# A token-mixing and expert-layer kernel: a new order of work for the first batch

## Chip, cores and metric

The kernel runs on one core of one Trainium2 chip. The metric is the device time of one execution in microseconds (us). Several executions of the same kernel are timed and the median is taken. One further thing is known of each kernel: a profile of one execution, with a record of every instruction on each engine. The engines are named as in the profile: PE (TensorE matmuls), PEld (its weight loads), DVE (VectorE), ACT (ScalarE), POOL (GpSimd) and SP (SyncE, which here only issues DMAs).

## What is computed

```python
X = np.fft.rfft(x, axis=1)                 # x: (8, 3008, 256)
Y = X * (filt_r + 1j * filt_i)[None]       # filters: (1505, 256)
y = np.fft.irfft(Y, n=3008, axis=1)        # (8, 3008, 256)
h = y.reshape(24064, 256) @ w_in           # w_in: (256, 2048)
g = h * (1 / (1 + np.exp(-beta * h)))      # beta: (2048,)
out = g @ w_out                            # (24064, 256), float32
```

## The kernel before

**The Fourier part.** 3008 is 47 times 64, so the transform is done in two stages of matmuls with tables. `t1` (94x96) is the first stage, `t2` (24 tables of 128x128) the second; the spectrum is multiplied with the filters on DVE; `t3` (24 tables of 128x128) and `t4` (96x94) take it back. `t3s` is `t3` with its two halves exchanged and a sign put on each row ("rotated"). The tables are computed on the chip: GpSimd writes index tiles (`iota`), DVE turns them into phases, ACT takes the sine.

**The expert part.** Blocks of 512 tokens, 47 of them. For each of 16 slices of the 2048 inner columns there is one step: two matmuls into `hps` (L719), one Silu on ACT (L728), and two steps later four matmuls into `acc` (L739). There are 752 steps. While the steps of one batch run, the Fourier stages of the next batches are put between them: a plan (`at`, L645) says at which step which matmul of which batch is issued (functions `s1`, `s2`, `s3`, `s4`).

**The first batch** has no steps to hide behind. It runs alone before step 0, in an order written out by hand (L298 to L542), with its own functions: `s1_0(g)` (first stage, 8 groups of 4 columns of x, evacuated into `aT` on DVE or ACT), `a0_turn` (PE transposes of `aT` into `a0`), `t3_part` (transposes of `t2` into `t3`), `t3_rotate` (from `t3` to `t3s`), `s2_0(n)` (second stage of unit n, and its two products `pq_t` with the filters on DVE, L423), `s3_0(n)` (back, evacuated into `zT`), `z_turn` (transposes into `zz0`), `f_0` and `s4_0` (last stage, evacuated into `ys[0]`). There are six units n, each 8 of the 24 tables by one half of the 256 columns. `spin` is a run of matmuls whose result nobody reads.

**Queues.** Each engine runs its instructions in the order of the program. The DMAs of x (float32 in memory, bfloat16 in SBUF) are issued by POOL, in the same order as its `iota`s and copies; so are half of the filter loads (`load_filters(nc.gpsimd, ...)`, L185), w_in (L480) and x of the next batch (`load_x`, L347). The other half of the filters, w_out (`load_wout`) and all later stores and loads are issued by SP. A filter half lands in 32 of 64 rows; `spread(n)` (two POOL copies, L455 and L456) makes the second 64 rows that the products of unit n need. The SP filter loads stand behind a tiny DMA `seen` (L189) that reads the second group of x.

**x in two transfers.** A batch of x is laid out as 94 rows of 32 times 256 values. Each load is two DMAs, of 80 and of 14 rows (L170 and L171, L351 and L352).

PSUM in this stage: `spsum` has 3 buffers of two banks (`bank2`), `tpsum` 2 buffers of one bank (`turn8`, `f_0`, `spin`). A matmul into a buffer waits until the engine that evacuates it is done.

Of the kernel before, what the change touches and what calls it, by code (L numbers as in the profile page):

```python
# [10 lines left out]
P = 128  # L11

ACT = mybir.ActivationFunctionType
ALU = mybir.AluOpType
ENG = mybir.EngineType
F32 = mybir.dt.float32
# [20 lines left out]
def kernel(  # L37
# [104 lines left out]
    def iota(tile_, pattern, base=0, ch=0):  # L142
        nc.gpsimd.iota(tile_, pattern=pattern, base=base, channel_multiplier=ch)
# [6 lines left out]
    ip = sp.tile([P, 1], I32, name="ip", tag="ip")  # L150
    warm = small("warm")
    nc.vector.memset(warm[:], 0.0)
    nc.scalar.activation(warm[:], warm[:], ACT.Sin)

    r_sr = ExitStack()
# [4 lines left out]

    r_sq = ExitStack()
    sq = rpool("setup_x", r_sq, bufs=1)
    x0 = sq.tile([NP, J, D], BF16, name="x0", tag="x0")
    xv0 = x[0].rearrange("(p j) d -> p j d", j=J)
    kc = sq.tile([P, NK, 2], I32, name="kc", tag="kc")
    cc = sq.tile([P, NK, 2], I32, name="cc", tag="cc")
    vi = sq.tile([P, NK, M], I32, name="vi", tag="vi")

    def load_x0(j0, j1):
        nc.gpsimd.dma_start(x0[:80, j0:j1, :], xv0[:80, j0:j1, :])  # L170
        nc.gpsimd.dma_start(x0[80:, j0:j1, :], xv0[80:, j0:j1, :])  # L171

    load_x0(0, 8)
    iota(ip[:], [[0, 1]], ch=1)
# [3 lines left out]
    iota(vi[:, :, :H], [[1, NK], [N1, H]])  # L178
    load_x0(16, 24)
    iota(vi[:, :, H:], [[1, NK], [-N1, H]], base=N1 * (M - 1))  # L180
    make_identity(nc, ident)
    load_x0(24, 28)
    load_x0(28, 32)
    for part in parts:
        load_filters(nc.gpsimd, *part)  # L185
    with nc.allow_non_contiguous_dma(reason="2048 values, once"):
        nc.sync.dma_start(beta_sb[:], moe_beta.rearrange("(fb fp) -> fp fb", fp=P))
    seen = sp.tile([1, 2], BF16, name="seen", tag="seen")
    nc.sync.dma_start(seen[:], x0[:1, 8, :2])  # L189
    for part in parts:  # L190
        load_filters(nc.sync, *part)

    def shift_and(name, sh, mask):
        t = small(name, I32)
        if sh:
# [47 lines left out]
    def s1_0(g, engines):  # L243
        ps = bank2([P, NDC, 512])
        for e in range(NDC):
            for i in range(MG):
                nc.tensor.matmul(
                    ps[:, e, i * KP : (i + 1) * KP],
                    lhsT=x0[:, g * MG + i, e * P : (e + 1) * P],
                    rhs=t1[:],  # L250
                    start=True,
                    stop=True,
                )
# [7 lines left out]
    def spin(j, n):  # L261
        ps = tpsum.tile([P, 512], F32, name="tps", tag="tps")
        for _ in range(n):
            nc.tensor.matmul(
                ps[:], lhsT=x0[:, j, :P], rhs=x0[:, j : j + 2, :], start=True, stop=True
            )

    def a0_turn(kg, e, on_act):
        tp = turn8()
# [22 lines left out]
    def turn_t4():  # L292
        tp = turn8()
        nc.tensor.transpose(tp[:KP, 0, :NP], t1[:], ident[:NP, :NP])
        nc.scalar.activation(t4[:], tp[:KP, 0, :NP], ACT.Copy)
        nc.gpsimd.tensor_scalar(t4[0:4], t4[0:4], 0.5, None, ALU.mult)

    t1v = t1[:].rearrange("p (k q) -> p k q", q=2)  # L298
    t2_half(0)
    for q in range(2):  # L300
        nc.vector.tensor_scalar_mul(t1v[:, :, q], sn[:NP], q_p[q][:NP])
    t2_half(1)
    s1_0(0, (False,))
    s1_0(1, (True,))
    spin(0, 3)
    t2_shift(0)
    t2_shift(1)
    nc.vector.memset(t2[:, 0, M : P : M - 1], 0.0)
    nc.scalar.activation(warm[:], ms[:], ACT.Silu)
    s1_0(2, (False,))  # L310
    s1_0(3, (True,))
    t3_part(0, True)
    turn_t4()
    v_i = shift_and("v_i", 5, 1)
    rot = (affine("rot0", v_i, 2.0, -1.0), affine("rot1", v_i, -2.0, 1.0))
    sgn = affine("sgn", c_i, -2.0, 1.0)
    c10 = sp.tile([P, P], BF16, name="c10", tag="c10")
    for c in range(2):
        nc.vector.tensor_copy(c10[:, c * M : (c + 1) * M], t2[:, 0, (1 - c) * M : (2 - c) * M])
    s1_0(4, (False,))  # L320
    s1_0(5, (True,))
    s1_0(6, (False,))
    s1_0(7, (False, True))
    t3_part(1, True)
    t3_rotate(1, KH, False)
    a0_turn(0, 0, False)
    a0_turn(1, 0, True)

    r_sq.close()

# [14 lines left out]
    wstage = {}  # L345

    def load_x(b, g):  # L347
        xv = x[b].rearrange("(p j) d -> p j d", j=J)
        t = xpool.tile([NP, JG, D], BF16, name="xg", tag="xg")
        js = slice(g * JG, (g + 1) * JG)  # L350
        nc.gpsimd.dma_start(t[:80], xv[:80, js, :])  # L351
        nc.gpsimd.dma_start(t[80:NP], xv[80:NP, js, :])  # L352
        xg[b, g] = t

    def load_wout(f0):
# [103 lines left out]
    def f_0(e, u, on_act):  # L459
# [14 lines left out]
            inv_scale,  # L474
        )

    spread(0)
    spread(1)
    spread(2)
    nc.gpsimd.dma_start(win_sb[:], moe_w_in.rearrange("(dc p) f -> p dc f", p=P))  # L480
# [8 lines left out]
    load_x(1, 3)  # L489
    load_wout(0)  # L490
    load_wout(WG)

    s2_0(0)
    t3_part(2, True)
    tp0 = turn8()
    nc.tensor.transpose(tp0[:, 0, :], c10[:], ident[:])
    nc.scalar.activation(t3s[:, 0, :], tp0[:, 0, :], ACT.Copy, scale=sgn[:])
    s2_0(1)
    a0_turn(2, 0, True)
    t3_rotate(KH, 2 * KH, True)  # L500
    s3_0(0)
    s2_0(2)
    a0_turn(0, 1, True)
    t3_rotate(2 * KH, NK, True)
    s3_0(1)
    s2_0(3)
    a0_turn(1, 1, True)
# [2 lines left out]
    a0_turn(2, 1, True)  # L510
    z_turn(0, 0, True)
    z_turn(0, 1, True)
    f_0(0, 0, True)
    f_0(0, 1, True)
    s3_0(3)
    s2_0(5)
    z_turn(0, 2, True)
    f_0(0, 2, True)
    f_0(0, 3, True)
    z_turn(0, 3, True)  # L520
    s3_0(4)
    f_0(0, 4, True)
    tiny = sp.tile([P, NFB], F32, name="tiny", tag="tiny")
    nc.gpsimd.tensor_tensor(tiny[:], beta_sb[:], beta_sb[:], ALU.mult)
    nc.gpsimd.tensor_scalar(tiny[:], tiny[:], 1e-12, None, ALU.is_lt)
    nc.gpsimd.tensor_scalar(tiny[:], tiny[:], 2e-6, None, ALU.mult)
    nc.gpsimd.tensor_tensor(beta_sb[:], tiny[:], beta_sb[:], ALU.add)
    f_0(0, 5, True)
    s3_0(5, True)
    f_0(0, 6, False)  # L530
    f_0(0, 7, True)
    z_turn(1, 0, False)
    z_turn(1, 1, True)
    s4_0(1, 0, False)
    z_turn(1, 2, False)
    s4_0(1, 1, True)
    z_turn(1, 3, False)
    nc.vector.reciprocal(rbeta_sb[:], beta_sb[:])
    scale_wout(0)
    scale_wout(WG)  # L540
    s4_0(1, 2, True)
    s4_0(1, 3, False)  # L542
    r_p0.close()
    r_sr.close()
    right.close()
# [14 lines left out]
    def s1(b, i, on_act):  # L560
        g, jj = divmod(2 * i, JG)
        if jj == 0:
            st["a1", b] = apool.tile([KP, JG, D], BF16, name="a1", tag="a1")
        ps = fpsum.tile([P, 512], F32, name="ps1", tag="f")
        nc.tensor.matmul(  # L565
            ps[:KP], lhsT=t1[:], rhs=xg[b, g][:, jj : jj + 2, :], start=True, stop=True
        )
        evac(st["a1", b][:, jj : jj + 2, :], ps[:KP], on_act)

# [218 lines left out]
```

## Time and profile before

| | |
|---|---|
| six runs, median (lowest to highest) | 791.58 us (789.74 to 793.6) |
| the profiled execution, its own time | 792.72 us |
| its span, first to last instruction | 790.9 us |
| PE, ACT, DVE, POOL busy, share of the span | 96%, 71%, 55%, 22% |
| first matmul of step 0 | 48.81 us |
| last first-batch DMA of x landed | 15.92 us |
| first spectrum product `pq_t` | 20.90 us |

The profile is read in stages. The time from 0 to 48.81 us is the first batch alone; from there on the steps run. The table of stretches gives for each stretch the busy time of every engine, the granted TensorE clock and the busy share of the 16 DMA engines. The chain is the line of work that ended last, each piece the one that released the next.

### The profile page before, as it was taken

What the parts mean: (1) busy time and instruction counts of PE and PEld (TensorE: products, weight loads), DVE (VectorE), ACT (ScalarE), POOL (GpSimd) and SP (SyncE); (2) the same over time, 40 slices, a digit from 0 to 9 for tenths busy, and PEclk for the clock granted to TensorE, in tenths of its full rate; (3) what the DMA queues carried; (4) which work ended last, traced back from release to release, by engine and by line L of the source; (5) the groups of instructions that cost most, each with busy time, mean ns of one, the idle gap of its engine ahead of it and who ended that gap; (6) DMA issues with size and microseconds to landing.
All of it is one profiled execution on the core that took longest, in us unless ns stands there. A gap on an engine that the chain in (4) does not pass through costs nothing.

```text
span 790.9 us, 15158 instructions
## 1 busy us (share of the span) xinstructions
PE 763.0 (96%) x5953; PEld 547.0 (69%) x6045; DVE 436.8 (55%) x683; ACT 561.8 (71%) x826; POOL 172.6 (22%) x195
## 2 busy tenths in 40 slices
PE   4789999999999999999999999999999999999997
PEld 4666767766677666776678666786667776676665
DVE  6754845676556765576655666566655566330100
ACT  4877877766667666767667766677666777777776
POOL 8925410233102321122201222012200222000000
PEclk9999999999999999999999999999999999999999
DMA  9948375441941339313581335803154211500101
GB/s 172 228 130 198 104 194 144 108 108 58 233 135 48 87 89 241 96 48 97 126 239 52 82 99 127 226 27 114 48 179 115 74 47 48 154 28 27 54 27 54
DMA packets 87530, 88.28 MB, mean 112 GB/s; under 512 B 6150, under 2 KB 78342, under 8 KB 87460
## 3 DMA queue, kind: packets, MB, share of 16 engines
q1 hardware_dynamic: 82420, 72.37, 30.7%
q0 software_dynamic: 5040, 14.95, 11.1%
q8 instruction: 47, 0.77, 0.4%
q14 instruction: 23, 0.19, 0.1%
HBM read 54.01 MB, written 46.66 MB: 127 GB/s over the span
## 4 chain that ended last, share of the span: by engine, by line
PE 93%; ACT 2%; DMA 2%; POOL 1%; issue 1%; DVE 1%; POOLq 0%; ACTq 0%
PE acc L739 42%; PE hps L719 38%; PE ps L565 3%; PE ps L632 3%; PE ps L610 3%; PE ps L581 2%; DMA a<-d 1%; DMA x<-in_x_dram 1%; ACT zz L113 1%; ACT a L113 0%; POOL x L170 0%; PE sps L432 0%; PE tps L386 0%; ACT t3s L288 0%; POOL x L171 0%
## 5 line engine op out<-in xcount | busy, mean ns | idle before, releaser
L728 ACT ACTIVATE gT<-hps,beta_sb 128x512 bf16<-128x512 f32 x752 | 516.7, 687 | 209.3 <-PE hps L719 188.5
L739 PE MATMUL acc<-wout_sb,gT 128*128 128x256 bf16 x3008 | 453.3, 272 | 2.5
L719 PE MATMUL hps<-y,win_sb 128*128 128x512 bf16 (+7 forms) x1636 | 428.2, 350 | 1.3 <-DVE y L117 1.0
L739 PEld LDWEIGHTS <-gT 128*128 128x128 bf16 x3008 | 287.5, 98 | 126.2 <-issue 1.2
L600 POOL TENSOR_TENSOR yh<-a_t,b_t 128x512 bf16<-128x512 f32 x84 | 106.3, 1266 | 415.0 <-DVE b_t L599 414.2
L719 PEld LDWEIGHTS <-win_sb 128*128 128x128 bf16 x1728 | 164.9, 98 | 25.3 <-issue 1.3
L115 DVE COPY ost<-acc 128x512 f32<-128x512 f32 x93 | 59.9, 685 | 146.9 <-PE acc L739 146.9
L115 DVE CAST a<-ps 96x512 bf16<-96x512 f32 x104 | 70.9, 685 | 51.9 <-PE ps L565 47.9
L595 DVE TENSOR_TENSOR a_t<-ps,fr_sb 128x512 f32<-128x512 f32 x84 | 58.1, 691 | 72.0 <-PE ps L581 70.9
L117 DVE TENSOR_SCALAR y<-ps 128x376 bf16<-128x376 f32 x104 | 55.9, 547 | 59.3 <-PE ps L632 59.1
L596 DVE SCALAR_TENSOR_TENSOR b_t<-ps,fi_sb 64x512 f32<-64x512 f32 x84 | 58.2, 692 | 1.1
L599 DVE TENSOR_TENSOR b_t<-ps,fi_sb 64x512 f32<-64x512 f32 x84 | 57.4, 683 | 1.1
L115 DVE CAST z<-ps 128x512 bf16<-128x512 f32 x72 | 49.3, 684 | 1.7 <-PE ps L610 0.8
L632 PEld LDWEIGHTS <-zz 96*128 96x128 bf16 x448 | 29.8, 98 | 22.9 <-DMA zz<-d 0.2
L565 PE MATMUL ps<-xg,t 94*96 94x512 bf16 x112 | 41.5, 381 | 0.6
L632 PE MATMUL ps<-t,zz 96*128 96x94 bf16 x448 | 34.7, 205 | 0.8
L581 PE MATMUL ps<-a,t 128*128 128x256 bf16 x168 | 32.1, 273 | 1.1 <-DMA a<-d 0.8
L610 PE MATMUL ps<-yh,t 128*128 128x256 bf16 x168 | 32.1, 273 | 0.6
L351 POOL DMA_DIRECT2D xg<-in_x_dram x28 | 15.2, 542 | 63.3 <-PE ps L565 63.3
L610 PEld LDWEIGHTS <-t 128*128 128x128 bf16 x168 | 16.3, 98 | 17.7
L581 PEld LDWEIGHTS <-t 128*128 128x128 bf16 x168 | 16.1, 98 | 16.0 <-issue 1.1
L565 PEld LDWEIGHTS <-t 94*96 94x96 bf16 x112 | 13.8, 123 | 10.5
(100 smaller groups left out, 204.8 us busy)
## 6 DMA issues: line engine op xcount, KB each, us to landing
out_dram<-ost SPq DMA_DIRECT2D x46, 512.0 KB, 3.0
d<-a SPq DMA_DIRECT2D x28, 384.0 KB, 4.4
a<-d SPq DMA_DIRECT2D x28, 384.0 KB, 5.3
d<-z SPq DMA_DIRECT2D x28, 384.0 KB, 3.7
zz<-d SPq DMA_DIRECT2D x28, 384.0 KB, 7.0
xg<-in_x_dram POOLq DMA_DIRECT2D x28, 320.0 KB, 5.8
ws<-in_moe_w_out_dram SPq DMA_DIRECT2D x4, 512.0 KB, 14.6
xg<-in_x_dram POOLq DMA_DIRECT2D x28, 56.0 KB, 5.8
```

Of the source, the lines that this page charges most:

```text
L115: nc.vector.tensor_copy(dst, src)
L565: nc.tensor.matmul(ps[:KP], lhsT=t1[:], rhs=xg[b, g][:, jj : jj + 2, :], start=True, stop=True)
L581: nc.tensor.matmul(ps[:, e, :], lhsT=t2[:, k0 + e, :], rhs=st["a2", b, g][:, kk + e, :], start=True, stop=True,)
L595: nc.vector.tensor_tensor(a_t[:], ps[:], fr_sb[:, ks, :], ALU.mult)
L596: nc.vector.scalar_tensor_tensor(b_t[:M], ps[M:], -1.0, fi_sb[M:, ks, :], ALU.mult, ALU.mult)
L599: nc.vector.tensor_tensor(b_t[M:], ps[:M], fi_sb[M:, ks, :], ALU.mult)
L600: nc.gpsimd.tensor_tensor(yh[:], a_t[:], b_t[:], ALU.add)
L610: nc.tensor.matmul(ps[:, e, :], lhsT=t3[:, 2 * i + e, :], rhs=yh[:, e, :], start=True, stop=True)
L632: nc.tensor.matmul(ps[:, e, :NP], lhsT=zz[:, j0 % JG + e, dc * P : (dc + 1) * P], rhs=t4[:], start=True, stop=True,)
L719: nc.tensor.matmul(hps[:, pos - t0 : pos - t0 + ln], lhsT=win_sb[:, dc, fb * P : (fb + 1) * P], rhs=ys[b][:, dc, n0 : n0 + ln], start=(dc ...
L728: nc.scalar.activation(gT[:], hps[:], ACT.Silu, scale=beta_sb[:, fb : fb + 1])
L739: nc.tensor.matmul(acc[tb // 2][:, tb % 2, :], lhsT=gT[:, tb * P : (tb + 1) * P], rhs=wout_sb[:, fb, :], start=(fb == 0 and tb % 2 == 0), ...
```

## The change

It leaves the steps as they are, but for one entry of the plan, and rewrites the first batch in these points:

- a bfloat16 tile `rest` of zeros; `spin(17)` on it ahead of all matmuls, and `spin(4)` where `spin(0, 3)` was;
- x in single DMAs of 96 rows (the last two rows are those of the next batch, and no matmul reads them), for the first batch and for all others but the last;
- the identity after the fourth x load; the fourth and fifth filter parts on POOL not ahead of the spreads but just before `spread(0)` and `spread(1)`; `seen` on SP reads `t2`, so that the SP filter loads start when `t2` is nearly done;
- the two writes of `t1` on ACT instead of DVE;
- the work on `beta` on DVE early, and `scale_wout` after the last x load on POOL;
- `t3_part(1)` and `t3_part(2)` earlier; the second of three `t3_rotate` on DVE, right before the products, the third stays on ACT;
- another order of `s3_0(3)`, `s2_0(5)`, `z_turn` and `f_0`; the last two `z_turn` become one `z_pair` into a two-bank buffer;
- in the plan of batch 1, the first `s2` at step 19 instead of 18.

```diff
+    rest = sp.tile([P, 512], BF16, name="rest", tag="rest")
+    nc.vector.memset(rest[:], 0.0)
...
+    def load_rows(t, b, j0, j1):
+        if b + 1 < B:
+            src = AP(x.tensor, x.offset + (b * S + j0) * D, [[J * D, KP], [D, j1 - j0], [1, D]])
+            nc.gpsimd.dma_start(t, src)
+        else:
...
     def load_x0(j0, j1):
-        nc.gpsimd.dma_start(x0[:80, j0:j1, :], xv0[:80, j0:j1, :])
-        nc.gpsimd.dma_start(x0[80:, j0:j1, :], xv0[80:, j0:j1, :])
+        load_rows(x0[:, j0:j1, :], 0, j0, j1)
...
+    load_x0(24, 28)
     make_identity(nc, ident)
-    load_x0(24, 28)
     load_x0(28, 32)
-    for part in parts:
+    for part in parts[:3]:
         load_filters(nc.gpsimd, *part)
...
-    seen = sp.tile([1, 2], BF16, name="seen", tag="seen")
-    nc.sync.dma_start(seen[:], x0[:1, 8, :2])
-    for part in parts:
-        load_filters(nc.sync, *part)
...
+    spin(17)
     t1v = t1[:].rearrange("p (k q) -> p k q", q=2)
+    for q in range(2):
+        nc.scalar.activation(t1v[:, :, q], sn[:NP], ACT.Copy, scale=q_p[q][:NP])
     t2_half(0)
-    for q in range(2):
-        nc.vector.tensor_scalar_mul(t1v[:, :, q], sn[:NP], q_p[q][:NP])
     t2_half(1)
     s1_0(0, (False,))
     s1_0(1, (True,))
-    spin(0, 3)
+    spin(4)
...
     nc.vector.memset(t2[:, 0, M : P : M - 1], 0.0)
+    seen = sp.tile([1, 2], BF16, name="seen", tag="seen")
+    nc.sync.dma_start(seen[:], t2[:1, 1, P - 2 :])
+    for part in parts:
+        load_filters(nc.sync, *part)
...
-    turn_t4()
...
+    nc.vector.reciprocal(rbeta_sb[:], beta_sb[:])
     s1_0(4, (False,))
     s1_0(5, (True,))
+    t3_part(1, True)
     s1_0(6, (False,))
+    turn_t4()
     s1_0(7, (False, True))
-    t3_part(1, True)
     t3_rotate(1, KH, False)
     a0_turn(0, 0, False)
     a0_turn(1, 0, True)
+    t3_part(2, True)
+    t3_rotate(KH, 2 * KH, False)
...
+    load_filters(nc.gpsimd, *parts[3])
     spread(0)
+    load_filters(nc.gpsimd, *parts[4])
     spread(1)
...
+    scale_wout(0)
+    scale_wout(WG)
 
     s2_0(0)
-    t3_part(2, True)
...
+    a0_turn(2, 0, True)
     s2_0(1)
-    a0_turn(2, 0, True)
-    t3_rotate(KH, 2 * KH, True)
+    t3_rotate(2 * KH, NK, True)
     s3_0(0)
...
-    t3_rotate(2 * KH, NK, True)
...
+    s3_0(3)
+    s2_0(5)
     f_0(0, 0, True)
     f_0(0, 1, True)
-    s3_0(3)
-    s2_0(5)
     z_turn(0, 2, True)
+    z_turn(0, 3, True)
     f_0(0, 2, True)
     f_0(0, 3, True)
-    z_turn(0, 3, True)
...
-            s23_steps(1, [o + r for r in (18, 21, 23, 26, 28, 30, 34, 36, 39, 41, 44, 46)], 5, 1)
+            s23_steps(1, [o + r for r in (19, 21, 23, 26, 28, 30, 34, 36, 39, 41, 44, 46)], 5, 1)
```

`z_pair(e, hh, engines)` does the transposes of two `z_turn`s into one buffer of `spsum`, and evacuates the two halves on the two engines given.

More of the change, by code (lines that the diff above doesn't have):

```diff
@@ L162 @@
     sq = rpool("setup_x", r_sq, bufs=1)
-    x0 = sq.tile([NP, J, D], BF16, name="x0", tag="x0")
-    xv0 = x[0].rearrange("(p j) d -> p j d", j=J)
+    x0 = sq.tile([KP, J, D], BF16, name="x0", tag="x0")
     kc = sq.tile([P, NK, 2], I32, name="kc", tag="kc")
@@ L167 @@
     vi = sq.tile([P, NK, M], I32, name="vi", tag="vi")
+    def load_rows(t, b, j0, j1):
[3 more added lines that the diff above has]
+        else:
+            xv = x[b].rearrange("(p j) d -> p j d", j=J)
+            nc.gpsimd.dma_start(t[:80], xv[:80, j0:j1, :])
+            nc.gpsimd.dma_start(t[80:NP], xv[80:NP, j0:j1, :])
     def load_x0(j0, j1):
-        nc.gpsimd.dma_start(x0[:80, j0:j1, :], xv0[:80, j0:j1, :])
-        nc.gpsimd.dma_start(x0[80:, j0:j1, :], xv0[80:, j0:j1, :])
+        load_rows(x0[:, j0:j1, :], 0, j0, j1)
     load_x0(0, 8)
@@ L248, in s1_0 @@
                     ps[:, e, i * KP : (i + 1) * KP],
-                    lhsT=x0[:, g * MG + i, e * P : (e + 1) * P],
+                    lhsT=x0[:NP, g * MG + i, e * P : (e + 1) * P],
                     rhs=t1[:],
@@ L259, in s1_0, with spin @@
                 evac(aTv[:, g, e], src[:, e], engines[e])
-    def spin(j, n):
+    def spin(n):
         ps = tpsum.tile([P, 512], F32, name="tps", tag="tps")
         for _ in range(n):
-            nc.tensor.matmul(
-                ps[:], lhsT=x0[:, j, :P], rhs=x0[:, j : j + 2, :], start=True, stop=True
-            )
+            nc.tensor.matmul(ps[:], lhsT=rest[:, :P], rhs=rest[:], start=True, stop=True)
     def a0_turn(kg, e, on_act):
@@ L319 @@
         nc.vector.tensor_copy(c10[:, c * M : (c + 1) * M], t2[:, 0, (1 - c) * M : (2 - c) * M])
+    tiny = sp.tile([P, NFB], F32, name="tiny", tag="tiny")
+    nc.vector.tensor_tensor(tiny[:], beta_sb[:], beta_sb[:], ALU.mult)
+    nc.vector.tensor_scalar(tiny[:], tiny[:], 1e-12, 2e-6, ALU.is_lt, ALU.mult)
+    nc.vector.tensor_tensor(beta_sb[:], tiny[:], beta_sb[:], ALU.add)
+    nc.vector.reciprocal(rbeta_sb[:], beta_sb[:])
     s1_0(4, (False,))
     s1_0(5, (True,))
+    t3_part(1, True)
     s1_0(6, (False,))
+    turn_t4()
     s1_0(7, (False, True))
-    t3_part(1, True)
     t3_rotate(1, KH, False)
@@ L347, in load_x @@
     def load_x(b, g):
[L348 to L352, printed above, removed]
+        t = xpool.tile([KP, JG, D], BF16, name="xg", tag="xg")
+        load_rows(t[:], b, g * JG, (g + 1) * JG)
         xg[b, g] = t
@@ L475, in f_0, with z_pair @@
         )
+    def z_pair(e, hh, engines):
+        tp = spsum.tile([P, 2, KH, P], BF16, name="sps", tag="sps")
+        for h in range(2):
+            for i in range(KH):
+                j0 = ((hh + h) * KH + i) * KP
+                nc.tensor.transpose(tp[:, h, i, :], zT[e][:, j0 : j0 + P], ident[:])
+        for h in range(2):
+            evac(zz0[:, (hh + h) * KH : (hh + h + 1) * KH, e * P : (e + 1) * P], tp[:KP, h], engines[h])
+    load_filters(nc.gpsimd, *parts[3])
     spread(0)
+    load_filters(nc.gpsimd, *parts[4])
     spread(1)
@@ L512 @@
     z_turn(0, 1, True)
+    s3_0(3)
+    s2_0(5)
     f_0(0, 0, True)
     f_0(0, 1, True)
-    s3_0(3)
-    s2_0(5)
     z_turn(0, 2, True)
+    z_turn(0, 3, True)
     f_0(0, 2, True)
     f_0(0, 3, True)
-    z_turn(0, 3, True)
     s3_0(4)
     f_0(0, 4, True)
[L523 to L527, printed above, removed]
     f_0(0, 5, True)
@@ L533 @@
     z_turn(1, 1, True)
+    z_pair(1, 2, (False, True))
     s4_0(1, 0, False)
-    z_turn(1, 2, False)
     s4_0(1, 1, True)
[L537 to L542, printed above, removed]
+    s4_0(1, 2, False)
+    s4_0(1, 3, True)
     r_p0.close()
@@ L565, in s1 @@
         nc.tensor.matmul(
-            ps[:KP], lhsT=t1[:], rhs=xg[b, g][:, jj : jj + 2, :], start=True, stop=True
+            ps[:KP], lhsT=t1[:], rhs=xg[b, g][:NP, jj : jj + 2, :], start=True, stop=True
         )
```

## Prediction

> **What bounds the kernel now.** I read the table of stretches first, because the shares over the span mix two stages.
>
> ```profile
> 15.00:20.00 5.00, 3.42 (x38) 3.05 (x39) 2.13 (x5) 1.72 (x3) 3.09 (x6) 0.68 1.12 235
> 20.00:25.00 5.00, 3.99 (x62) 3.55 (x61) 4.10 (x4) 4.38 (x7) 4.77 (x5) 0.98 1.10 230
> 35.00:40.00 5.00, 4.02 (x52) 3.80 (x50) 2.35 (x2) 3.28 (x5) 3.87 (x9) 0.78 1.05 191
> 45.00:50.00 5.00, 3.51 (x47) 2.51 (x45) 3.57 (x6) 2.46 (x4) 2.55 (x2) 1.00 0.00 0
> 100.00:760.00 660.00, 655.48 (x5024) 467.94 (x5104) 369.17 (x575) 466.78 (x685) 112.72 (x113) 1.00 0.39 106
> ```
>
> Columns: stretch, length, then busy us of PE, PEld, DVE, ACT, POOL, the granted clock, DMA share, GB/s. From 100 to 760 us PE is busy 655.48 of 660 at clock 1.00: no edit here removes a matmul of the steps, so that stage stays. In the first 50 us no engine is full; there the order of work decides. So second comes the chain in order of time (start, us, what):
>
> ```profile
> 9.50 0.51 POOL x L170
> 10.02 5.90 DMA x<-in_x_dram
> 16.05 0.52 PE sps L247 x8
> 16.59 0.57 DVE aT L115
> 17.18 0.49 ACT aT L113
> ...
> 23.63 1.22 ACT t3s L288 x2
> ...
> 26.68 1.22 ACT t3s L288 x2
> ...
> 34.19 1.71 PE sps L432 x16
> ...
> 41.02 0.91 PE sps L432 x16
> ...
> 47.82 0.95 DVE y L117
> 48.81 0.59 PE hps L719 x2
> ```
>
> Read: POOL issues x until 10.02, the last x lands 5.90 later, then DVE and ACT evacuate, then ACT carries the chain (with four rotations), then PE at half speed (1.71 against 0.91 for the same 16 matmuls), and a tail of 6.9 us from the last `s3_0` to step 0. Third, the timeline around two waits:
>
> ```profile
> 18.64 1.01 PE L272 MATMUL tps<-ident,aT 128*128 128x128 bf16 x8 [0.33 <-ACT t L113]
> 19.84 1.03 POOL L455 COPY fr_sb<-fr_sb 64x1024 f32<-64x1024 f32 x1
> 21.96 0.61 PE L272 MATMUL tps<-ident,aT 128*128 128x128 bf16 x8 [0.54 <-ACT t L113]
> 68.55 0.38 PE L581 MATMUL ps<-a,t 128*128 128x256 bf16 x2 [0.84 <-DMA a<-d]
> ```
>
> The first spread starts only at 19.84, because POOL was still issuing filters, and POOL then copies without a gap to 35.89. The last row is the one stall of the early steps: 0.84 us at step 18.
>
> **x.** Ahead of the last x DMA, four issues of 14 rows go (0.53 + 0.51 + 0.86 + 0.51); the last issue then ends near 7.6 instead of 10.65. The data do not come that fast: with x alone on the queues the stretches of 4 to 8 us moved about 200 GB/s, so 1.57 MB (two more rows of 94 are 2%) take 7.9 us from 3.3, and the first group landed about 0.9 us after its share had moved; so x is in at 12.1 instead of 15.92. Here the Trainium skill ("DMA: Bandwidth & Descriptors", Anatomy of one DMA) gives each such DMA a fixed 2.0 us beside its bytes: five fewer would then be worth 10 us. The rows show the DMA engines already at share 1.03 to 1.10 at 5 to 8 us, so the fixed parts overlap; I take the issue and the bytes. This costs the filters: the SP ones start at about 11 instead of 8.44.
>
> **DVE and ACT to the end of the first stage.** The index `ip` comes 0.53 earlier, and the two `t1` writes (0.91) leave DVE for ACT, which is idle then (ACT waits 1.46 at 6.87). The zero memset precedes `ip` and is hidden. So `t2` is ready at 11.53 - 1.3 = 10.2. From there DVE is the late engine: `aT` 0.85, small ops and `c10` 0.7, four new ops on `beta` about 0.8 (POOL took 0.22 to 0.27 each), `aT` 0.9, 0.85 and 0.55: 14.85, then ACT's half 0.5: **15.35 against 17.67**. Of 3.8 us that x is earlier, 2.3 are used.
>
> **POOL.** `t4` is turned on ACT at 13.95; POOL scales it (0.47), issues two filter DMAs (0.59 each) and spreads from **15.7, against 19.84**. Two issues of filters (1.2) come between spreads 0 and 1, two of x (1.1) go: the last spread ends at 32.05 against 35.89. The filters must be there. After x is through at 11.2, the 3.15 MB of both halves take 13.7 us at the 230 GB/s of the rows above: the first pairs (128 KB each) land near 14 to 15, the last between 25.8 and 26.7, and spread 4 needs them at 27.15. That is the thinnest cover of the sum. Without it each us of lateness goes to the products, after 1.7 us of slack (below). The moved w_out scaling (2 x 1.89 on POOL) lies behind the last spread and is needed only at step 2; its cost is nothing, as DVE and ACT don't wait for it.
>
> **Rotations.** One pair leaves ACT, where it stood on the chain (1.22), for DVE. A DVE rotation took 0.34, so 0.65, and the first product comes at 17.2 (20.90 before). The rule of the skill against this: "SBUF — State Buffer", section "SBUF: two separate sides", says of the port pair that DVE and GpSimd share that a DVE instruction in a two-port mode and a GpSimd one block each other whole. By it each rotation waits for a spread copy of 1.04, and the first product is at 18.5; the row of 4.09, a DVE op on 128x48 that took 0.97 until an `iota` of POOL ended, agrees. The unit after it waits for its spread until 21.15 either way, so the sum keeps nothing of this.
>
> **ACT to the last `s3_0`.** With ACT ops of 1024 elements 0.92 apart: `a0` 15.95, `t3` 16.9, `t3s` 17.8, `a0` 18.4, rotation 19.3 to 20.55, `zT(0)` to 21.5, `a0` to 22.4, `zT(1)` (waits for spread 1) to 24.1, `a0`, `zT(2)`, `a0` to 27.2, two `zz` to **29.1 (33.7 before)**. With `s3_0(3)` and `s2_0(5)` ahead of `f_0`, ACT's wait of 1.22 at 35.94 and most of 0.57 at 37.53 go; `zT(3)` 30.0, two `y` 31.0, two `zz` 32.9, two `y` 33.9, `zT(4)` 35.1; PE does `s3_0(5)` at 34.9 to **35.8, against 41.9**. The last product is ready at 33.2 (the 1.7 of slack). The tail I work out again with `z_pair`: 6.9, as before, since the last `zz` on ACT waits for DVE's. Step 0 so starts at 42.7, 6.1 earlier. x of batch 1 lands last near 42, and its first use of that part is six steps later.
>
> **Clock.** A 128x512 matmul took 0.63 at 8.95 (cold, though the clock column shows 1.00 before its first record) and 0.38 at 48.81. PE worked from 7.71 and the x matmuls went from 281 to 206 ns at 13.1. 17 spins cost 7.3 us cold (0.43 each); started at 1.3 they end between 6.7 and 8.6, where t1 and x are ready at 6.1; DVE reaches the first `aT` at 7.5. Gain or loss on the path: -0.5 to +1.1, taken at 0. The clock fell at 16.9 and 33.9, each time after a stretch with PE waiting. The new order has such stretches too (29 to 33). A cold window cost, at 34 to 37, 1.0 (16 matmuls of L432 in 1.91 for 0.91), 0.45 (L418, 1.06 for 0.61) and 0.34 (L386, 0.95 for 0.61); I take **one, at 1.2**, the rest lying beside ACT; ends 0 and 3.5 (two).
>
> **Step 19.** The stall of 0.84 goes. But three `s2` then come in six steps, and DVE needs 2.07 for each, so the third `s3` can come 0.2 to 0.3 late: +0.6 net.
>
> **Sum:** 6.1 - 1.2 + 0.6 = 5.5. The profiled execution took 792.72 (span 790.9): it would be 787.2 (785.4). It lay 1.14 above the median, so the median goes from 791.58 to 786.1.
>
> **Rivals.** *The clock holds:* no cold window, 6.7 saved, 784.9. For: the spins bring it up early. Against: PE still waits for ACT. *The filters are late:* x first means 3.1 MB of filters from 11 us on, and a filter DMA of 256 KB took 9.6 to 14.0 to land. If spread 4 starts 4 us late, minus the slack, 2.2 are lost: 788.3. For: the SP loads start 2.6 later, and the DMA share is above 1 throughout. Against: what lands earlier frees the queue for them. In the same place falls the case that x is not earlier at all, because bytes and not issues set it. *The other side, the clock stays down:* if transposes and zero operands don't hold the clock, the stage from 18.4 on has 37 groups of 8 matmuls at 0.86 (the cold row at 35.59) = 32 us, plus some 3 us of evacuation that nothing hides: step 0 at 53.4, 4.6 later, less the 0.6 of step 19: 795.6. It decides from about 60% of the stretch 18 to 43 cold. The skill ("TensorE: Matmul & The Clock Gate", Part 4) says that transposes don't count as busy; the rows speak against it: transposes took 1.01 at 18.64 and 0.61 at 21.96, and 43 to 48 is half transposes at clock 1.00.[...]
>
> **Chances.** Forecast 0.48; clock holds 0.20; filters late 0.20; clock down 0.06; else 0.06. 0.3% (2.4 us) is about what a measurement can tell from no change. Faster: the first two and 0.6 of the third, 0.80. Within: the rest of it and most of the unnamed, 0.13. Slower: 0.07. The range reaches from the warm case with a short spin (-0.5), no late `s3` (-0.25) and `beta` ops at half their price (-0.4), 783.8, to filters late with one cold window more (+1.2), 789.5.
>
> **What would show it.** Right: `t2` copies done near 10.2, x in by 12.5, first spread before 16.5, first product near 17.3, step 0 at 43 to 44, no wait of L581 on a DMA. Wrong: x still landing at 15; POOL's spreads waiting for DMAs; clock 0.50 in more than one window after 20; step 0 later than 46; or steps that run slower than 742.1 us from first to end.

## The result, and the profile after

| | before | changed |
|---|---|---|
| median of all runs (lowest to highest, runs) | 790.79 us (788.4 to 796.68, 66) | 786.95 us (785.44 to 789.52, 29) |
| the profiled execution, its own time | 792.72 us | 787.16 us |
| its span | 790.9 us | 785.4 us |
| first matmul of step 0 | 48.81 us | 42.37 us |
| from there to the end of the span | 742.1 us | 743.0 us |

The ratio is 0.9952, with the interval 0.9942 to 0.9962: 3.8 us faster. The spans of the profiled executions differ by 5.5 us, the number of the forecast. The 1.7 between the two is the first thing to explain: the profiled execution of before lay 1.9 us above the median of its 66 runs, that of the changed kernel 0.2 above its own.

The table of stretches of the changed kernel, with the columns as before:

```profile
15.00:20.00 5.00, 4.51 (x56) 4.23 (x53) 4.92 (x7) 3.24 (x5) 4.77 (x7) 0.66 1.16 239
35.00:40.00 5.00, 4.36 (x74) 3.82 (x70) 2.57 (x5) 3.53 (x7) 3.02 (x2) 1.00 1.07 215
45.00:50.00 5.00, 5.00 (x27) 2.94 (x26) 2.61 (x4) 3.77 (x8) 0.00 (x0) 0.85 0.63 182
100.00:760.00 660.00, 655.48 (x5023) 468.02 (x5104) 368.13 (x572) 466.31 (x683) 103.15 (x96) 1.00 0.39 106
```

Read: at 15 to 20 us all three of DVE, ACT and POOL have gained work that used to come later (DVE 4.92 for 2.13, POOL 4.77 for 3.09); 45 to 50 belongs to the steps now. The stretch at half clock at 15 to 20 is still there. That of 35 to 40 is gone (1.00 for 0.78), but a new one stands at 43.5 to 46.8, inside the steps (0.85 in the third row). In the long stretch PE is busy for 655.48 us in both.

The chain in order of time (start, us, what):

```profile
10.26 0.09 DVE aT L115
...
12.07 0.19 DVE beta_sb L329
12.28 0.25 DVE rbeta_sb L330
12.54 2.14 DVE aT L115 x3
...
20.32 1.22 ACT t3s L290 x2
...
31.50 1.94 ACT zz L113 x2
...
33.81 0.90 PE sps L443 x16
...
42.37 0.59 PE hps L732 x2
```

Read: before, the landing of x ended the first stage (5.90 of DMA on the chain). Now DVE does, with the small operations on `beta` right on the chain. One pair of rotations on ACT is left where two stood, and the 16 matmuls of the last `s3_0` take 0.90, not 1.71.

The timeline around the edits:

```profile
1.23 5.97 PE L268 MATMUL tps<-rest 128*128 128x512 bf16 x17 [1.23 <-DVE rest L154]
7.03 0.85 PE L251 MATMUL sps<-t,x 94*128 94x96 bf16 x16
15.92 1.03 POOL L466 COPY fr_sb<-fr_sb 64x1024 f32<-64x1024 f32 x1
15.99 2.20 DVE L292 TENSOR_SCALAR t3s<-t,rot 128x512 bf16<-128x512 bf16 x2
18.12 1.21 DVE L434 TENSOR_TENSOR pq_t<-sps,fr_sb 128x1024 bf16<-128x1024 f32 x1
19.34 1.03 POOL L466 COPY fr_sb<-fr_sb 64x1024 f32<-64x1024 f32 x1
28.49 1.03 POOL L466 COPY fr_sb<-fr_sb 64x1024 f32<-64x1024 f32 x1 [1.24 <-DMA fr_sb<-in_filt_r_dram]
64.14 0.38 PE L594 MATMUL ps<-a,t 128*128 128x256 bf16 x2 [0.25 <-DMA a<-d]
```

Read: the spins end at 7.20, and the x matmuls run warm at once. The first spread is 3.9 us earlier, and the second starts at 19.34. The rotations on DVE take 2.20 while POOL copies. The fifth spread (number 4) waits 1.24 us for its filters. The stall of the early steps has moved with the plan entry and is 0.25.

### The profile page after: what moved, and what is told of

It reads as the page before. It is cut to its first block, busy times and chain, and to the rows that moved or that the text cites. A ratio compares the mean times of both kernels' runs of the same rounds, so it can differ in the third digit from the quotient of the medians.

```text
span 785.4 us, 15141 instructions
## 1 busy us (share of the span) xinstructions
PE 765.7 (97%) x5971; PEld 546.4 (70%) x6063; DVE 438.1 (56%) x686; ACT 562.3 (72%) x827; POOL 155.7 (20%) x162
## 4 chain that ended last, share of the span: by engine, by line
PE 94%; DVE 2%; ACT 2%; issue 1%; DMA 1%; POOL 0%; POOLq 0%; ACTq 0%
PE acc L752 43%; PE hps L732 39%; PE ps L578 3%; PE ps L645 3%; PE ps L623 3%; PE ps L594 2%; DMA a<-d 1%; PE sps L443 1%; ACT zT L113 0%; ACT zz L113 0%; DVE aT L115 0%; PE tps L397 0%; DVE y L117 0%; DVE u L226 0%; PE tps L274 0%
## 5 line engine op out<-in xcount | busy, mean ns | idle before, releaser
L623 PEld LDWEIGHTS <-t 128*128 128x128 bf16 x168 | 16.3, 98 | 17.7
L594 PEld LDWEIGHTS <-t 128*128 128x128 bf16 x168 | 16.1, 98 | 15.6 <-issue 0.5
L173 POOL DMA_DIRECT2D xg<-in_x_dram x24 | 12.4, 519 | 56.5 <-PE ps L578 56.5
```

The costliest lines, as they stand in the source:

```text
L594: nc.tensor.matmul(ps[:, e, :], lhsT=t2[:, k0 + e, :], rhs=st["a2", b, g][:, kk + e, :], start=True, stop=True,)
L623: nc.tensor.matmul(ps[:, e, :], lhsT=t3[:, 2 * i + e, :], rhs=yh[:, e, :], start=True, stop=True)
```

## The experiments

**Before again.** The kernel before, with nothing changed, to have a second trace of it and to see how much of the forecast belongs to one execution.

> The kernel before, unchanged, run again for a second trace and for the noise of the comparison. In the trace shown, its own time was 792.72, 1.9 above the median of 66 runs (790.79), while the trace of the changed kernel (787.16) lies 0.2 above its median (786.95). Theory A (the sum of the forecast is right, and the gain of 5.5 was counted from a slow execution of before): ratio 1.000 within 0.1%, step 0 starts at 46.5 to 48.0 instead of 48.81, or the stage after it is shorter than 742.1. Rival B (a term of the sum is too large): step 0 again at 48.8 and the stage after it 742.1, within 0.3.

Measured: 791.72 us beside 792.16 for other executions of the same kernel, measured with it; ratio 0.9997 [0.998, 1.0014]. The profiled execution has a span of 788.4, and step 0 at 46.81 instead of 48.81. First a piece of the chain of the first trace of before, then the chain of this one:

```profile
31.78 1.93 ACT zz L113 x2
```

```profile
11.29 6.76 DMA fr_sb<-in_filt_r_dram
...
31.39 1.93 ACT zz L113 x2
...
33.69 0.91 PE sps L432 x16
...
46.81 0.59 PE hps L719 x2
```

The same 16 matmuls of L432 take 0.91, where the first trace of before shows 1.71, and the granted clock stays at 1.00 from 22 us on, where that trace had 0.50 from 34 to 37. Both traces have the clock at half near 17 to 21. Step 0 is 2.0 earlier here. Of this, 0.4 was there before the stretch at half clock began (the two `zz` start at 31.78 and at 31.39); the other 1.6 is what the stretch at 34 to 37 cost. It is not a property of the kernel: one execution has it and the next has not. The forecast counted its gain from the execution that had it. The clock is not all that differs between executions, though: of 27 more executions of before, the five with a mean clock of 1.000 took 790.53 to 792.45 us, and one at 0.999 took 788.86. Between 8 and 31 us it is POOL that carries this chain (issues, the filters' landing, the spreads), not ACT.

**The changed kernel again.** Nothing changed, to have a second trace of this kernel too.

> The changed kernel, unchanged, for a second trace. Theory A2 (what each execution has of cold clock windows, one to two at places that differ, moves step 0 and the early steps by about 1.2 each; the rest is fixed): end of the first stage 15.2 to 15.9, last product ready 34.5 to 36.0, step 0 at 42.4 to 44.0, time 785.5 to 788.5. Rival (the first trace was typical to the tenth): step 0 at 42.4 within 0.3.

Measured: 787.47 us, ratio to the kernel before, measured with it, 0.9937 [0.9918, 0.9956]; the profiled execution's own time 787.15, span 785.4, as in the first trace. Its stretches and its chain:

```profile
35.00:40.00 5.00, 4.10 (x56) 3.98 (x54) 1.31 (x3) 2.75 (x5) 2.95 (x2) 0.77 1.07 215
45.00:50.00 5.00, 5.00 (x30) 2.92 (x29) 3.10 (x5) 4.53 (x9) 0.00 (x0) 1.00 0.34 89
```

```profile
31.92 1.94 ACT zz L113 x2
...
34.37 1.71 PE sps L443 x16
36.08 0.63 PE tps L473 x8
36.70 1.26 PE sps L443 x16
...
44.39 0.59 PE hps L732 x2
```

Here the clock is at half at 34 to 37 and whole in the steps. Step 0 comes at 44.39, 2.0 later than in the first trace of the same kernel; from step 0 to the end it takes 741.0, 2.0 less. The two spans are equal because each has one stretch at half clock where PE is on the chain. Here too 0.4 of the 2.0 is older than the stretch (`zz` at 31.50 and at 31.92), so that the stretch cost 1.6; the 2.0 in the steps contain the stall of 0.25, which this trace has not. Both traces also have a stretch at half clock near 16 to 20.

So the traces are best compared at two points that lie ahead of 33 us: the start of the second spread on POOL, and the start of the first two `zz` on ACT.

| kernel | end of the first stage | second spread | first two `zz` | step 0 | half clock at 33 to 38 | from `zz` to step 0 |
|---|---|---|---|---|---|---|
| before | 17.67 | 22.02 | 31.78 | 48.81 | yes | 17.0 |
| before again | 16.77 | 21.73 | 31.39 | 46.81 | no | 15.4 |
| x alone | 14.94 | 17.25 | 28.36 | 43.79 | no | 15.4 |
| changed | 15.19 | 19.34 | 27.60 | 42.37 | no | 14.8 |
| changed again | 15.70 | 19.78 | 28.00 | 44.39 | yes | 16.4 |
| x in two transfers | 16.50 | 20.55 | 28.98 | 44.48 | yes | 15.5 |
| no spin | 16.20 | 19.98 | 28.73 | 43.51 | no | 14.8 |
| rotation on ACT | 15.53 | 19.52 | 28.92 | 43.69 | no | 14.8 |
| old order | 15.81 | 19.73 | 27.95 | 42.92 | no | 15.0 |
| `seen` on x | 15.24 | 19.50 | 27.73 | 43.94 | yes | 16.2 |
| step 18 | 15.51 | 20.43 | 28.65 | 43.44 | no | 14.8 |
| filled waits | 15.62 | 20.05 | 28.27 | 44.40 | yes | 16.1 |
| w_out late | 15.77 | 20.45 | 28.68 | 44.96 | yes | 16.3 |
| w_out late, early rotation | 15.12 | 20.95 | 29.18 | 45.58 | yes | 16.4 |

Read: with a whole clock the way from `zz` to step 0 is 15.4 us in the kernels of before, 14.8 in the changed ones and 15.0 with the old order. A stretch at half clock adds 0.7 to 1.6. In eight of the eleven traces of changed kernels the `zz` start 8.22 to 8.26 after the second spread, with a stretch at half clock at 16 to 20 (*changed*, *changed again*) or without (*old order*, *filled waits*), so that stretch costs nothing that can be seen. The three others are *x in two transfers* (8.4), *no spin* (8.8) and *rotation on ACT* (9.4). In the changed kernel, then, the `zz` and with them step 0 follow the second spread. And the second spread moves between executions: *changed*, *changed again* and *step 18*, which have the same first batch, have it at 19.34, 19.78 and 20.43, and `zz` at 27.60 to 28.65. A difference of 1 us between single traces is not yet one between kernels.

**x alone.** In the kernel before, only the loads of the first batch are changed, with the place of the identity between them:

```diff
-    x0 = sq.tile([NP, J, D], BF16, name="x0", tag="x0")
+    x0 = sq.tile([KP, J, D], BF16, name="x0", tag="x0")
...
     def load_x0(j0, j1):
-        nc.gpsimd.dma_start(x0[:80, j0:j1, :], xv0[:80, j0:j1, :])
-        nc.gpsimd.dma_start(x0[80:, j0:j1, :], xv0[80:, j0:j1, :])
+        src = AP(x.tensor, x.offset + j0 * D, [[J * D, KP], [D, j1 - j0], [1, D]])
+        nc.gpsimd.dma_start(x0[:, j0:j1, :], src)
...
+    load_x0(24, 28)
     make_identity(nc, ident)
-    load_x0(24, 28)
```

> The kernel before with x of the first batch in single 96-row DMAs and the fourth of them ahead of the identity; nothing else changed. Theory A (earlier x passes on only in part, since t2 stays at 11.5 on DVE and POOL keeps its ten filter DMAs ahead of the first spread): x in 1.5 to 2.5 earlier, end of the first stage 15.5 to 16.3 instead of 16.8 to 17.7, first spread 17.5 to 18.5 instead of 19.6 to 19.8, step 0 1.0 to 2.0 earlier, 789.2 to 790.2. Rival D (bytes, not issues): within 0.5 of 791.

Measured: 788.64 us, ratio 0.9957 [0.9934, 0.9979] against 792.09 for the kernel before, measured with it. That is 3.45 us (by the interval, 1.7 to 5.2), where the whole change gives 4.62 against the same 792.09 (the two intervals overlap). In the trace it is above the 1.0 to 2.0 expected: step 0 comes 3.0 earlier than in the second trace of before. The profiled execution was a fast one of its kernel (786.73). The chain:

```profile
14.45 0.49 ACT aT L113
...
20.21 1.22 ACT t3s L288 x2
...
23.25 1.22 ACT t3s L288 x2
```

The first stage ends at 14.94, without spins, and the first spread is at 15.07 (19.55 in the second trace of before). POOL no longer carries the chain; ACT does, with two pairs of rotations on it. The five small DMAs of 14 rows had taken POOL 0.53 + 0.51 + 0.86 + 0.51 + 0.64 = 3.05 us to issue.

**x in two transfers.** In the changed kernel the first batch is loaded as before, in DMAs of 80 and 14 rows.

```diff
-        load_rows(x0[:, j0:j1, :], 0, j0, j1)
+        nc.gpsimd.dma_start(x0[:80, j0:j1, :], xv0[:80, j0:j1, :])
+        nc.gpsimd.dma_start(x0[80:NP, j0:j1, :], xv0[80:NP, j0:j1, :])
```

> The changed kernel with x of the first batch in two DMAs of 80 and 14 rows again; all else as changed. Theory A (the issue on POOL held x back, by 2.4 before the last DMA): x in near 14 instead of 11.5 to 12, end of the first stage 16.2 instead of 15.19, filters of POOL later by up to 2.6, so that spread 4 waits more than the 1.24 now; 788 to 789. Rival D (bytes set x's landing and DVE the end of the first stage, so that issues were hidden): within 0.5 of 786.95.

Measured: 788.43 us, ratio 0.9956 [0.9942, 0.9971]. The last issue ends at 10.70 instead of 7.13, the first stage at 16.5 instead of 15.2 to 15.7. It is 1.1 and 2.2 us slower than two other changed kernels measured with it (787.32 and 786.27, below), while its ratio is close to that of the changed kernel (0.9952). In the trace the `zz` start at 28.98, 0.3 to 1.4 later than in the three traces of the changed first batch. Between nothing and 2 us, then, and less than x gives alone: here DVE's work ends the first stage, so x that comes later finds some cover. Put the other way, all the other parts without this one still give 3.73 us (792.16 to 788.43), about as much as x alone. The gains of the parts overlap and don't add up.

**No spin.** The changed kernel without its zero-tile matmuls.

```diff
-    spin(17)
...
-    spin(4)
```

> The changed kernel without the 17 and the 4 matmuls on the zero tile. Theory A (chain: at this place DVE is late, so the clock of the first matmuls costs little; the forecast took the spins at 0, with bounds -0.5 and +1.1): 786.9 to 787.8, ratio to before 0.995 to 0.996, x matmuls at 281 ns until 10 to 13 us, first-stage end at most 0.8 later than 15.19. Rival C (the clock does most of the gain): 789.5 or more, step 0 3 us later than 42.37.

Measured: 787.32 us, ratio 0.9945 [0.9924, 0.9966]: no difference to the changed kernel in the time. In the timeline, though:

```profile
6.66 1.46 PE L251 MATMUL sps<-t,x 94*128 94x96 bf16 x16 [6.66 <-DMA x<-in_x_dram]
9.00 1.46 PE L251 MATMUL sps<-t,x 94*128 94x96 bf16 x16 [0.88 <-DMA x<-in_x_dram]
```

16 of the x matmuls take 1.46 instead of 0.85. The first stage ends at 16.2 instead of 15.2 to 15.7, and the `zz` start 8.8 after the second spread instead of 8.2. So the spins do warm PE, and that is worth 0.5 to 1 us in the trace; the times don't resolve it. The spins have a price too: the 17 take 5.48 to 6.71 us in the traces, and where they end late, DVE waits for the x matmuls behind them (0.48 us in *changed again*, 0.72 in *w_out late*).

**Rotation on ACT.** The second pair of `t3_rotate` goes back to ACT.

```diff
-    t3_rotate(KH, 2 * KH, False)
...
     s2_0(1)
-    t3_rotate(2 * KH, NK, True)
+    t3_rotate(KH, 2 * KH, True)
     s3_0(0)
...
     a0_turn(0, 1, True)
+    t3_rotate(2 * KH, NK, True)
```

> The changed kernel with the second rotation pair on ACT again, at its old place. Theory A (the pair stood on ACT's chain, 1.22): first product about 0.9 earlier than 18.12, since DVE no longer waits for POOL's copies there (the pair took 2.20 in the changed trace, 0.65 forecast), but step 0 0.7 to 1.2 later; 787.6 to 788.2. Rival F (POOL's spreads pace the products and ACT's waits swallow the pair): step 0 within 0.3, 786.6 to 787.3.

Measured: 787.97 us, ratio 0.995 [0.9933, 0.9968]. The first spread is at 16.11, the first product at 18.8: not earlier, since it now waits for PE. The chain:

```profile
20.67 1.22 ACT t3s L290 x2
...
23.81 1.22 ACT t3s L290 x2
```

The second pair is back on the chain, and the way from the second spread to the `zz` is 9.4 instead of 8.2. This trace has two early stretches at half clock, one behind the other (11.5 to 18.5 us), and its products start 0.7 late, so not all of the 1.2 need be the rotation; the 1.22 on the chain is. With x alone the chain has the same two pairs. The times don't tell this kernel from the changed one.

**Old order.** The old order of `f_0`, `s3_0(3)`, `s2_0(5)` and `z_turn`, all else as changed.

```diff
+    f_0(0, 0, True)
+    f_0(0, 1, True)
     s3_0(3)
     s2_0(5)
-    f_0(0, 0, True)
-    f_0(0, 1, True)
     z_turn(0, 2, True)
-    z_turn(0, 3, True)
     f_0(0, 2, True)
     f_0(0, 3, True)
+    z_turn(0, 3, True)
```

> The changed kernel with the old order of s3_0(3), s2_0(5), z_turn and f_0. Theory A (the order takes ACT's waits of 1.22 and 0.57 away): step 0 1.2 to 1.8 later, 788.2 to 788.8; ACT waits about 1 on s3_0(3). Rival H (in the trace of before these waits came from a PE at half speed, and at full speed the order is worth nothing): step 0 within 0.4.

Measured: 787.69 us, ratio 0.9945 [0.9924, 0.9967]. The span is 783.9, the shortest of all traces here, with no stretch at half clock in the first 50 us. From the `zz` to step 0 it takes 14.97 us, and 14.77 to 14.79 in the four traces of the new order with a whole clock: the new order is worth 0.2. ACT waits 0.41 for `s3_0(3)` here, and 0.41 in the changed kernel. The wait of 1.22 that the new order was to remove, in the first trace of before, comes again in the second trace of the changed kernel, which has the new order:

```profile
35.94 1.02 ACT L113 ACTIVATE zT<-sps 128x1024 bf16<-128x1024 f32 x1 [1.22 <-PE sps L432]
36.11 1.02 ACT L113 ACTIVATE zT<-sps 128x1024 bf16<-128x1024 f32 x1 [1.22 <-PE sps L443]
```

Both stand beside PE at half clock. The wait belongs to the clock and not to the order.

**Filled waits.** Spins in the two places where the first trace of the changed kernel lost its clock: at the end of the first stage, and just before step 0.

```diff
     s1_0(7, (False, True))
+    spin(3)
...
     s4_0(1, 1, True)
+    spin(3)
     s4_0(1, 2, False)
     s4_0(1, 3, True)
+    spin(3)
```

> The changed kernel with three groups of three more matmuls on the zero tile: after s1_0(7), before s4_0(1, 2), and before step 0, where PE waits. Theory A (clock: a cold window of 3.4 falls where PE waited, and cost 1.2 to 1.6 each; one at 15.8 to 19.1 and one at 43.5 to 46.8, inside the steps): granted clock 1.00 there, 785.2 to 786.2. Rival J (the window comes elsewhere, or the fill delays PE by what it is long): 786.7 to 787.8.

Measured: 787.01 us, ratio 0.9938 [0.9917, 0.9959]. The clock stays whole at both filled places. A stretch at half clock comes between them, at 33 to 37:

```profile
30.00:33.00 3.00, 1.78 (x31) 1.55 (x29) 2.33 (x2) 2.68 (x5) 2.90 (x4) 1.00 1.08 218
33.00:36.50 3.50, 2.65 (x29) 2.54 (x29) 2.38 (x3) 2.09 (x5) 3.38 (x5) 0.59 1.05 212
```

Filling these two waits gave no time. Since two traces of one kernel already differ in such stretches, one trace doesn't show that the spins moved it.

**`seen` on x.** The SP filter loads start when the second x group has landed, as before, not at `t2`.

```diff
-    nc.sync.dma_start(seen[:], t2[:1, 1, P - 2 :])
+    nc.sync.dma_start(seen[:], x0[:1, 8, :2])
```

> The changed kernel with the SP filter loads released by the second group of x again, as before, instead of by t2. Theory A (filters beside x delay x; x first is worth more than filters first): last x lands 1.5 to 3 later, end of the first stage about 1 later, 787.5 to 788.5, and the wait of spread 4 on its filters (1.24) goes. Rival E (total bytes are the same, and the products wait for filters, not for x): 786 to 786.9.

Measured: 786.27 us, ratio 0.9938 [0.9913, 0.9962]. The SP loads start at 9.5 instead of 10.6; the first spread is at 15.86; spread 4 still waits, 1.65 us. x takes 6.2 us from issue to landing in the median, not 5.6, but the first stage ends at 15.24, against 15.19. No gain from the gating by `t2` is seen.

**w_out late.** The loads of w_out are moved from the filters' time to behind `s3_0(2)`, gated by a small DMA that reads `zT`, and `scale_wout` with them.

```diff
     load_x(1, 3)
-    load_wout(0)
-    load_wout(WG)
-    scale_wout(0)
-    scale_wout(WG)
...
     s3_0(2)
+    seen2 = sp.tile([1, 2], BF16, name="seen2", tag="seen2")
+    nc.sync.dma_start(seen2[:], zT[0][:1, 64:66])
+    load_wout(0)
+    load_wout(WG)
+    scale_wout(0)
+    scale_wout(WG)
```

> The changed kernel with the first two loads of w_out released by zT of the first half (a tiny DMA ahead of them on SP) instead of straight after the filters. Theory A2 (w_out on SP's queue takes half of the DMA engines while the last filters of POOL's queue are waited for: spread 4 waited 1.24 to 1.65, and step 0 came 7.8 to 8.9 after the last product in every trace): no wait of spread 4 on a DMA, last product about 1.3 earlier, step 0 0.5 to 1.3 earlier, 785.7 to 786.5. Rival K (the slack of the last product covers this wait, as the forecast had it): last product earlier, but step 0 and the time the same within 0.4.

Measured: 789.02 us, ratio 0.9953 [0.9934, 0.9973], no better than the changed kernel. The wait of spread 4 is gone, as meant, and the DMA share falls from 1.08, of which 0.45 were SP's queue, to 0.82:

```profile
25.00:30.00 5.00, 4.27 (x70) 3.76 (x67) 4.01 (x5) 4.68 (x6) 4.78 (x8) 1.00 0.82 131
```

But spread 4 starts at 28.41, against 28.49 with the wait: POOL gets there no earlier, since the second copy of spread 0 had waited 0.75 for a filter, and the second spread started at 20.45. The last product ends at 34.48, against 34.56. So this trace alone doesn't show what the wait of spread 4 costs. The table does: spread 4 starts at 28.41 here, at 28.49 in the changed kernel and, after a wait of 1.64, at 29.60 in *filled waits*, and each time the `zz` start 8.2 to 8.3 after the second spread. The late filters of spread 4 are not what holds step 0. From step 0 to the end this trace takes 742.9, with a stall of 1.36 at step 19.

**w_out late, early rotation.** As the last, and the second pair of rotations straight behind the first, ahead of the transposes of `aT`.

```diff
     t3_rotate(1, KH, False)
+    t3_rotate(KH, 2 * KH, False)
     a0_turn(0, 0, False)
     a0_turn(1, 0, True)
     t3_part(2, True)
-    t3_rotate(KH, 2 * KH, False)
```

> As e11, and the second rotation pair on DVE right after the first, ahead of the evacuation of a0, where POOL copies nothing yet. Theory A2 (the pair took 2.20 because it waited for POOL's copies[...]): the pair takes 0.7, the first product comes 0.2 to 0.6 earlier than 18.12, the first evacuation of a0 0.7 later; time within 0.4 of e11. Rival L (a0 is the later one for the chain on ACT and PE): 0.5 to 0.9 slower than e11.

Measured: 787.81 us, ratio 0.9955 [0.9935, 0.9975]; its profiled execution took 791.72, 3.9 above that. The four rotations take 1.11 together, ahead of the first copy. But the first spread waited 1.73 us for filters, to 17.54, and the first product came at 18.60. This trace has three stretches at half clock (14 to 18, 35 to 38 and 45 to 48), the most of all. No gain over the changed kernel is seen; whether the rotation's place gives a part of a microsecond stays open.

**Step 18.** The plan of batch 1 keeps its first `s2` at step 18.

```diff
-[o + r for r in (19, 21, 23, 26, 28, 30, 34, 36, 39, 41, 44, 46)]
+[o + r for r in (18, 21, 23, 26, 28, 30, 34, 36, 39, 41, 44, 46)]
```

> The changed kernel with the first s2 of batch 1 at step 18 again. Theory A: the wait on the load of a2 is 0.84 to 1.1 instead of 0.25, the time +0.6, 787.3 to 787.7. Rival I (the later step only crowds DVE, and what the stall costs is given back at steps 24 to 28): within 0.2 of 786.95, and from step 17 to step 40 the same length within 0.2.

Measured: 788.08 us, ratio 0.996 [0.9938, 0.9982]. The stall at step 18 is 0.22, where the first trace of before had 0.84. At step 18 the four traces show 0.84, 0.27, 0.22 and none; at step 19 the ten traces show 0.25, 1.42, 1.36, 1.16 and six times none. With either step the wait on the loads of `a` is there in some executions and not in others.

The first batch of this kernel is that of the changed one, and yet step 0 comes 1.1 later than in the first trace. The chain:

```profile
12.84 6.86 DMA fr_sb<-in_filt_r_dram
...
20.43 1.04 POOL fr_sb L466
```

A filter that lands at 19.70 holds up the second spread. The second copy of spread 0 had waited 0.84 for a filter before that.

## Why the prediction was right, and where its steps were not

The time is in the range, 0.85 us above the number, and the sign is right. The sum, 5.5, is the difference of the two spans. But its terms were not all what they were put at, and it was counted from an execution that was 1.9 us above its kernel's median; in the medians the gain is 3.8. That the number missed by no more than 0.85 is partly luck: the 66 executions of before have a median 0.8 below that of the six from which the forecast started.

**x, DVE, POOL, to the first spread: right.** `t2` was expected at 10.2, and its memset is at 10.29. End of the first stage: 15.35 expected, 15.19 measured. First spread: 15.7 and 15.92. Last `s3_0`: 35.8 and 35.95. Step 0: 42.7 and 42.37. Of the two prices for the small DMAs, the issue time was about 3 us; the fixed 2.0 us that the Trainium skill ("DMA: Bandwidth & Descriptors", Anatomy of one DMA) gives for one DMA, added up over five, were 10 us. *x alone* gave 3.0 in the trace and 3.45 in the time.

**What part gives it: not foreseen.** I expected 1 to 2 us of x alone. In the times it gives 3.45 of 4.62 us, and the rest without it gives 3.73: the parts overlap, and none of them is the cause by itself. The traces say where the time goes. From the second trace of before to the traces of the changed first batch, the second spread starts 1.3 to 2.4 earlier (21.73; 19.34 to 20.43). The way from there to the `zz` is 1.4 shorter (9.66; 8.22 to 8.26), about what the pair of rotations took on ACT (1.22). The way from the `zz` to step 0 is 0.6 shorter; 0.2 of that is the order, and for the rest `z_pair` is the candidate, which was not run alone. The spins (0.5 to 1) may do little more than pay back what the change itself puts on DVE: x alone, without spins, ends the first stage at 14.94, before the changed kernel's 15.19, whose chain has the four `beta` operations (0.17 + 0.19 + 0.25 and more, from 11.66 to 12.53) on it. That last step is read from the chain; the kernel with `beta` left on POOL was not run.

**Rotations: the skill's rule agrees, and it costs nothing.** I took 0.65 for the pair on DVE and 17.2 for the first product; "SBUF — State Buffer" (SBUF: two separate sides) gave 18.5. The pair took 2.20 under two copies of POOL, and the product came at 18.12. In five other traces about one copy fell on it, and it took 1.22 to 1.41; ahead of the copies two pairs took 1.11. The sum had put nothing on it, because the next unit waits for its spread anyway, and that was right: the `zz` come 8.2 after the second spread with 2.20 as with 1.22.

**Filters: late, and covered only in part.** "The thinnest cover" was too thin. Spread 4 waited 1.24 us, in every trace of a changed kernel with its w_out loads in place between 0.7 and 1.65. The last product ended at 34.56 instead of 33.2. The slack of 1.7 took it, as worked out. What the forecast took as in time are the filters of the first two spreads. In *step 18* they were not, and step 0 came 1.1 later.

**New order: the step that failed.** The forecast let "ACT's wait of 1.22 at 35.94 and most of 0.57 at 37.53 go", about 1.8. These waits were the trace of a half-speed PE at 34 to 37, not of the order: with PE at half speed the new order has the same 1.22, and at full speed both have 0.41. *Old order* puts the new one at 0.2.

**Clock: the base had such a stretch too.** "One, at 1.2" was taken off the new kernel. Between the `zz` and step 0 a stretch at half clock costs 0.7 to 1.6, and in the first steps 1.3 to 2.0 (743.0 and 742.9 from step 0 to the end, in *changed* and *step 18*, against 741.0 to 741.6 without one and with a stall of 0.27 or none). The changed kernel had one of these in each of its two traces, so the size was fair. But before had one in the trace from which the forecast started, and its 1.6 was credited to the order. From the second trace of before (step 0 at 46.81) the same 42.7 is 4.1 earlier, and the same sum gives 4.1 - 1.2 + 0.6 = 3.5, near the measured 3.8.

**Step 19: not shown.** From step 0 to the end the traces take 741.0 when there is no stall and no half clock in the steps, 742.1 in the first trace of before (stall 0.84) and 741.6 in the second (0.27). So a stall does cost about what the forecast put on it. That moving the entry by one step removes it is not shown: four of ten traces at step 19 have a stall, and three of four at step 18.

**Clock stays down: excluded.** Between 21.5 and 780 us the clock is at half in no more than two pieces of about 3.4 us in any trace.

What stays open: what decides whether a stretch at half clock comes and where. The Trainium skill ("TensorE: Matmul & The Clock Gate", Part 1) has the clock follow PE's activity over a free-running window of about 3.4 us, so that the same kernel meets it at another phase each time; the length of the stretches and their places fit that, but no run here varies the phase (filling two of PE's waits didn't settle it; keeping PE busy in all waits after 20 us was not tried). Open too is any difference of less than about 1.5 us between the changed kernels, whose medians lie between 786.27 and 789.02 with intervals of 0.15 to 0.25% to each side. None beats the changed kernel by more than that. And several parts were never run alone: `t1` on ACT, `beta` on DVE, the place of the fourth and fifth filter parts, the scaling of w_out, `z_pair`, and the single DMAs of the later batches.

## What to carry over

Before a gain is worked out from one trace, see whether its base holds a disturbance that the next execution won't have: here one stretch of 3.4 us at half clock was worth 1.6 of 790.9 us, and two traces of the same kernel differ by it. Compare traces at a point that lies ahead of the disturbance. Count the issue time of small DMAs on the engine that issues them: five of 14 rows took 3.05 us of POOL, and taking them out alone gave 3.45 us. When a change has several parts, run the cheapest alone, and the rest without it: here the rest gave 3.73 us and the whole 4.62, so the gains of parts that lie on the same wait don't add up.

## What the runs showed of the hardware

- The granted clock falls to 0.50 in pieces of about 3.4 us, none to three of them in the first 50 us (in one trace two follow each other), and at other places in the next execution of the same kernel. Matmuls then take twice their time (16 of L443: 1.71 for 0.90).
- The matmuls on a tile of zeros, 17 in 5.97 us, do warm PE: x matmuls after them run at 0.85 for 16, without them at 1.46. The clock column shows 1.00 in both cases, so in the first microseconds the time of a known matmul tells more than the column.
- Two DVE rotations of 512 columns under two POOL copies took 2.20, and 1.22 where one copy fell on them (*w_out late*); a pair of 448 columns, while POOL only issued DMAs, took 0.71.
- With the w_out loads taken out of the way, the DMA share fell from 1.08 to 0.82 at 25 to 30 us, and spread 4 no longer waited. An earlier wait for a filter (0.75, in spread 0) stood in that trace; *step 18*, with the w_out loads in place, has one of 0.84 there, so it need not come from the move.
